# Attention and two feed-forward blocks: the first block's second layer in seven products instead of eight

## The chip, the cores and the metric

The kernel runs on one core of a Trainium2 chip. The metric is the device time of one execution in microseconds; 961.36 us is the median of three runs (958.15, 961.36 and 961.68).

## The reference

Four batches of 448 tokens, 12 heads of 64: sigmoid attention gives x, 1792 tokens by 768. Two feed-forward blocks follow, all in float32.

```python
scores = scale * np.matmul(q, k.transpose(0, 1, 3, 2)) - np.log(S)
attn = 1.0 / (1.0 + np.exp(-scores))
x = np.matmul(attn, v)                       # reshaped to 1792 x 768
h = x @ moe_w_in                             # layer 1: 768 -> 2048
g = h - np.tanh(h)
x = g @ moe_w_out                            # layer 2: 2048 -> 768
h = x @ moe2_w_in                            # layer 3: 768 -> 2048
g = np.maximum(h, 0.0) + alpha * np.minimum(h, 0.0)
out = g @ moe2_w_out                         # layer 4: 2048 -> 768
```

## The kernel before

**Numbers.** A float32 product is made of float16 halves: every operand is split into a high part, the value times a power of two rounded to float16, and a low part, what the rounding left. `split` (line 271) writes both: the high part on ACT or DVE, as the planner likes, the low part on DVE alone. Three matmuls (`PASSES`: high by high, high by low, low by high) stand for one. A matmul takes 128 by 128 weights and 448 columns of activations (one batch). The tokens are worked in two halves `sb` of 896.

**Weights.** They arrive as float64 words. `words` (line 311) makes float32 of a unit of six 128 by 128 tiles with three DVE instructions out of a `stage` tile that GpSimd's queue (POOL) loads; the halves go by POOL to a scratch in DRAM (`to_scratch`), and SyncE (SP) fetches them when PE wants them (`fetch`). Layers 1 and 2 (`w1`, `w2`) are converted unit by unit (`convert`). For layers 3 and 4 (`w3`, `w4`) `convert_quarter` (line 344) takes four units, the blocks 21, 22, 11 and 12 of one quarter `q` of the matrix, forms four sums on DVE (`tt`) and writes seven scratch tiles, since these layers use Strassen's method in Winograd's form: a 2 by 2 block product takes seven products instead of eight (`SEQ` is their order), the sums of activations being made by `entry` (line 591) and `exits` (line 674).

**Layers.** Layer 1: `product` adds up 36 matmuls into one of four PSUM tiles `ps0` to `ps3` in turn, and `bend` (line 551) makes g of it; its last reader of the PSUM tile is a COPY_PREDICATED on DVE. `lagged` runs half 0 ahead of half 1. After a half's sixteenth row a scale is formed from the maxima (`scale_of`), and `split_act` splits g into 16 tiles `sG`. Layer 2 has 12 products of 96 matmuls, each copied out of PSUM once by ACT and squared once for the scale. Layers 3 and 4 have 1008 matmuls each, layers 1 and 2 have 1152 each. Layer 4 writes three banks (`YB`) and three others (`ZB`) alternately; one of either three lies in `ps2`.

**Order.** `Plan` keeps every instruction as a node with a cost, an engine, what it reads and writes. `deadlines` works back from PE's fixed sequence, and `run` (line 104) places nodes engine by engine by that deadline, hands out 51 SBUF slots of 128 by 896 float32, and fixes the order; `window` and `keep` hold a node back. Costs (`act`, `vec`, `MM`, and `MB` for bytes moved) are constants of the program. Every engine then works through its own sequence and waits where an operand isn't there. All instructions go through one helper, so that the profile names line 210 for nearly all of them; they are told apart by operation, names and shape.

Of the kernel before, what the change touches and what calls it, by code (L numbers as in the profile page):

```python
# [19 lines left out]
T2 = 2 * S  # L20
# [20 lines left out]
LAG = 4  # L41
# [4 lines left out]
class Node:  # L46


    def __init__(self, n, engine, cost, emit, reads, writes, lat, window, keep):
        self.n, self.engine, self.cost, self.emit = n, engine, cost, emit  # L50
        self.touched = list(dict.fromkeys(r[0] for r in (*reads, *writes)))
        self.lat, self.window, self.keep = lat, window, keep
        self.before, self.after = set(), []
        self.late = self.end = None
        self.left, self.ready = 0, 0.0


class Plan:
# [3 lines left out]
    MB = 1.0 / 0.33  # L62
# [7 lines left out]
    def add(self, engine, cost, emit, reads=(), writes=(), lat=0.12, window=None, keep=1.0):  # L70
        node = Node(len(self.nodes), engine, cost, emit, reads, writes, lat, window, keep)
# [25 lines left out]
    def deadlines(self):  # L97
        total = sum(n.cost["T"] for n in self.nodes if n.engine == "T")
        for n in reversed(self.nodes):
            length = min(n.cost.values())  # L100
            ends = [a.late - (0.0 if n.engine == "T" and a.engine == "T" else n.lat) for a in n.after]
            n.late = min(ends, default=total + 8.0) - length - (n.cost.get("M", 0.0) * self.MB)

    def run(self):
# [20 lines left out]
        while done < len(self.nodes):  # L125
            picked = None
            base = order[turn].late if turn < len(order) else 1e9
            for e in engines:
# [10 lines left out]
                for n in waiting[e]:  # L139
# [5 lines left out]
                    key = n.late + (6.0 if len(n.engine) > 1 and e == "V" else 0.0)  # L145
# [79 lines left out]
def body(ctx: ExitStack, tc, qkd, vd, w1, w2, w3, w4, al, out):  # L225
# [8 lines left out]
               for m in (2, 3) for pr in range(1, 8) for q in range(NQ)}  # L234
    scratch.update({u: dr_pool.tile([128, 2 * UC], F16, name=f"scr_{u}") for u in range(2 * NU)})
# [35 lines left out]
    def split(dst, src, reads, scale, pick_dst, pick_src, n, regions, extra=(), ptr=0, keep=1.0):  # L271
# [9 lines left out]
        def low(e):  # L281
# [4 lines left out]
            [(dst, "h", r) for r in regions], keep=keep)  # L286
# [18 lines left out]
    def load_stage(i, queue):  # L305
# [3 lines left out]
        add(queue, {queue: 0.06 if queue == "S" else 0.6, "M": 0.786}, f, [], [(f"#stage{i % NSTAGE}",)])  # L309

    def words(i, name, after=()):
# [3 lines left out]
        def w():  # L315
# [5 lines left out]
            [*s, *after], whole(name), keep=8.0)  # L321
# [9 lines left out]
    def to_scratch(key, name, scale):  # L331
# [5 lines left out]
            parts(dst, (0,)), [("#scr", key)])  # L337
# [6 lines left out]
    def convert_quarter(m, q):  # L344
# [71 lines left out]
    def load_pair(i, halves=1):  # L416
        name = f"sqk{i}"
        n = T2 // halves
        for j in range(halves):
            add("S", {"S": 0.06, "M": 0.46 / halves},  # L420
                lambda e, j=j: SP.dma_start(out=slot(name)[:, j * n:(j + 1) * n], in_=qkd[i][:, j * n:(j + 1) * n]),
                [], [(name, j)] if halves == 2 else whole(name), window=60.0, keep=8.0)
# [6 lines left out]
    def load_values(g):  # L429
        add("S", {"S": 0.06, "M": 0.46}, lambda e: SP.dma_start(out=slot(f"sv{g}"), in_=vd[g]),  # L430
            [], [(f"sv{g}", 0)], window=60.0, keep=8.0)
# [60 lines left out]
    def weight_units(m, n0, nk):  # L492
        return sorted({n // UN for n in range(n0, n0 + nk)})

    turn = [0]

    def fetch_units(m, u, again):
        fetch((m if m < 2 else 1) * NU + u, f"sW{m},{u}")

    def product(m, n0, nk, act_of, sb, chunk):  # L500
# [3 lines left out]
        for c0 in range(0, nk, chunk):  # L504
            ks = range(c0, c0 + chunk)

            def f(e, ks=ks):
                for k in ks:
                    u, r = divmod(n0 + k, UN)
                    t = slot(f"sW{m},{u}").bitcast(F16)[:, 0:2 * UC]  # L510
                    w = t.rearrange("p (a k c) -> p a k c", a=2, k=UN)[:, :, r, :]
                    for i, j in PASSES:
                        for b in range(2):
                            PE.matmul(p[:, b, 0:S], w[:, i], act_of(k, sb, b)[1][:, j],
                                      start=(k == 0 and (i, j) == (0, 0)),
                                      stop=(k == nk - 1 and (i, j) == (1, 0)))
# [427 lines left out]
```

## Time and profile before

| | us |
|---|---|
| three runs | 958.15, 961.36, 961.68 |
| the profiled execution | 957.92 |
| its span, first to last instruction | 955.9 |
| layer 1, 2, 3, 4 begin | 131.4, 349.6, 567.9, 761.0 |

The profile is of one execution. A row by form gives the busy time of a group of like instructions and the mean of one; neighbours on an engine overlap a little, so that busy time divided by the count is what one more instruction costs. A window gives each engine's busy time in a stretch. The stretches of the layers follow from PE's sequence: 1008, 1008 and 1152 matmuls make up exactly the 3168 that the timeline has from 349.57 on.

### The profile page before, as it was taken

How to read it: one execution, taken by the hardware profiler on the slowest of the kernel's cores; microseconds unless marked ns; L12 is line 12 of the kernel's file. 1: busy time of each engine (PE TensorE's matmuls, PEld its weight loads, DVE VectorE, ACT ScalarE, POOL GpSimd, SP SyncE). 2: the span in 40 equal slices, each digit the busy share in tenths (PEclk: the TensorE clock that was granted, in tenths of full speed). 3: DMA queues.
4: the chain of work that ended last, by engine and by line, in shares of the span. 5: the costliest groups of instructions: out<-in, count | busy, mean ns of one | idle time of the engine just before them, and what ended most of it. 6: DMA issues, size and time to landing. Idle time of an engine off the chain costs nothing. (4 is left out here: it accounts for less than half of the span.)

```text
span 955.9 us, 13508 instructions
## 1 busy us (share of the span) xinstructions
PE 943.6 (99%) x5280; PEld 464.7 (49%) x5280; DVE 708.7 (74%) x878; ACT 593.0 (62%) x739; POOL 87.6 (9%) x163
## 2 busy tenths in 40 slices
PE   7999999999999999999999999999999999999998
PEld 2333345555555555555555555455555455555554
DVE  5779889999988999957999999643782479792000
ACT  7999859999999998512543347765663476271000
POOL 0011220011100000111223220100000000000000
PEclk9999999999999999999999999999999999999999
DMA  9962883455331123586768983733223345443441
GB/s 352 412 253 96 276 298 103 161 182 192 133 122 50 34 90 108 182 281 215 265 232 326 384 308 121 247 117 125 92 65 102 130 149 177 154 143 122 161 128 58
DMA packets 48287, 170.75 MB, mean 179 GB/s; under 512 B 6112, under 2 KB 9440, under 8 KB 48224
## 3 DMA queue, kind: packets, MB, share of 16 engines
q1 hardware_dynamic: 32544, 88.10, 27.8%
q0 software_dynamic: 15680, 81.80, 23.5%
q8 instruction: 41, 0.67, 0.3%
q14 instruction: 22, 0.18, 0.1%
HBM read 129.77 MB, written 40.11 MB: 178 GB/s over the span
## 5 line engine op out<-in xcount | busy, mean ns | idle before, releaser
L210 PE MATMUL ps<-slot,slot 128*128 128x448 f16 (+2 forms) x4704 | 890.8, 369 | 2.2 <-ACT slot L210 1.6
L210 PEld LDWEIGHTS <-slot 128*128 128x128 f16 (+2 forms) x4896 | 444.6, 98 | 448.1 <-issue 33.5
L210 ACT ACTIVATE slot<-slot 128x896 f32<-128x896 f32 (+3 forms) x193 | 171.9, 903 | 141.0 <-DVE slot L210 103.9
L210 ACT ACTIVATE slot<-slot,sc 128x896 f16<-128x896 f32 (+1 forms) x164 | 164.0, 1030 | 61.2 <-PE ps L210 23.8
L210 DVE SCALAR_TENSOR_TENSOR slot<-slot,sc,slot 128x896 f16<-128x896 f32 (+1 forms) x122 | 132.6, 1138 | 5.6 <-ACT slot L210 5.4
L210 DVE SCALAR_TENSOR_TENSOR slot<-slot,slot 128x768 f16<-128x768 f32 (+2 forms) x113 | 108.9, 977 | 30.4 <-ACT slot L210 28.5
L210 DVE SCALAR_TENSOR_TENSOR slot<-stage,slot 128x768 int32<-128x768 int32 x128 | 120.7, 956 | 1.6
L210 DVE SCALAR_TENSOR_TENSOR slot<-ps,sc,slot 128x896 f32<-128x896 f32 (+1 forms) x50 | 48.3, 978 | 90.2 <-ACT slot L210 47.4
L210 ACT ACTIVATE slot<-ps 128x896 f32<-128x896 f32 x64 | 57.4, 909 | 62.1 <-PE ps L210 42.2
L210 ACT ACTIVATE slot<-ps,sc 128x896 f32<-128x896 f32 (+1 forms) x56 | 46.7, 837 | 74.2 <-PE ps L210 72.2
L210 ACT ACTIVATE slot<-ps,cst 128x896 f32<-128x896 f32 x84 | 79.4, 1015 | 4.8 <-PE ps L210 4.0
L210 DVE TENSOR_TENSOR slot<-slot,slot 128x768 f32<-128x768 f32 (+2 forms) x82 | 73.9, 933 | 10.0 <-ACT slot L210 9.7
L210 DVE SCALAR_TENSOR_TENSOR slot<-slot,nalpha,slot 128x448 f32<-128x448 f32 x64 | 41.0, 681 | 40.0 <-ACT slot L210 40.0
L210 POOL DMA_DIRECT2D scr<-slot x88 | 48.4, 550 | 216.0 <-DVE slot L210 176.0
L210 ACT ACTIVATE slot<-slot,cst 128x896 f32<-128x896 f32 x64 | 66.4, 1040 | 1.8 <-DVE ps L210 0.5
L210 PE MATMUL ps<-slot 64*128 64x448 f16 (+1 forms) x576 | 57.4, 359 | 6.0 <-ACT slot L210 5.9
L210 POOL DMA_DIRECT2D stage<-w x60 | 34.0, 567 | 292.8 <-DVE slot L210 286.0
L210 DVE TENSOR_TENSOR slot<-ps,slot 128x896 f32<-128x896 f32 x24 | 26.1, 1088 | 37.4 <-ACT slot L210 25.7
L210 DVE TENSOR_SCALAR slot<-stage 128x768 int32<-128x768 int32 x64 | 35.4, 557 | 11.1 <-DMA scr<-slot 8.1
L210 PEld LDWEIGHTS ps<-slot,slot 128*64 128x64 f32 (+1 forms) x384 | 20.1, 135 | 38.6 <-issue 36.0
L210 DVE COPY_PREDICATED slot<-slot,ps 128x896 f32<-128x896 int32 x32 | 38.0, 1187 | 0.1
L210 DVE SCALAR_TENSOR_TENSOR ps<-ps,sc,slot 128x896 f32<-128x896 f32 x32 | 36.9, 1152 | 0.0
(22 smaller groups left out, 129.1 us busy)
## 6 DMA issues: line engine op xcount, KB each, us to landing
slot<-scr SPq DMA_DIRECT2D x160, 384.0 KB, 3.7
stage<-w POOLq DMA_DIRECT2D x60, 768.0 KB, 5.1
scr<-slot POOLq DMA_DIRECT2D x88, 384.0 KB, 5.1
slot<-qk SPq DMA_DIRECT2D x23, 448.0 KB, 9.0
slot<-v SPq DMA_DIRECT2D x12, 448.0 KB, 9.0
out_t<-slot SPq DMA_DIRECT2D x24, 224.0 KB, 2.3
stage<-w SPq DMA_DIRECT2D x4, 768.0 KB, 10.9
slot<-qk SPq DMA_DIRECT2D x2, 224.0 KB, 2.7
```

Source lines behind the costliest of these rows:

```text
L210: return lambda *args, **kw: self.tc.keep_in_program_order(f(*args, **kw))
```

## The change

Layer 2 takes the seven products. `w2` is laid out in blocks and converted by `convert_quarter(1, q)`, which writes 28 scratch tiles instead of 16; each half of the tokens fetches 28 instead of 16. For `w2` and `w3` the sums of weight blocks are no longer made on DVE: ACT negates a block in place (`negate`) and a DMA on POOL's queue adds one SBUF tile to another (`plus`, `accum_op`), 32 such DMAs; `w4` keeps DVE. `exits` now also serves g: 16 differences of blocks per half on DVE, and 28 split tiles instead of 16. `multiply_out` is layer 4's loop made a function that layer 2 uses too, with 1008 matmuls; out of PSUM go 12 half-size copies on ACT, 9 half-size additions on DVE and 12 half-size squares per half. A product of layer 1 now covers two rows of 128 features and one batch instead of one row and two batches. The planner gets longer latencies for DMAs, a slightly higher rate of bytes, and new windows and reserves.

```diff
-LAG = 4
+AHEAD = {1: (0, 1, 3, 0), 2: (19, 22, 0, 20), 3: (27, 50, 7, 42)}
+CHAIN = {1: 5, 2: 1, 3: 4}
+MOVED = (False, False)
+LAG, KEEP_W, KEEP_F, KEEP_P, WIN_F, WIN_O, WIN_P, SPARE_V, WIN_Q = 4, 6, 4, 7, 16, 31, 39, 12, 51
+WSUM = (True, True, False)
...
-    MB = 1.0 / 0.33
+    MB = 1.0 / 0.36
...
-                    key = n.late + (6.0 if len(n.engine) > 1 and e == "V" else 0.0)
+                    key = n.late + (SPARE_V if len(n.engine) > 1 and e == "V" else 0.0)
...
-                n.end = moved + 1.2
-            n.emit(e)
+                n.end = moved + n.lat
...
-        add(queue, {queue: 0.06 if queue == "S" else 0.6, "M": 0.786}, f, [], [(f"#stage{i % NSTAGE}",)])
+        add(queue, {queue: 0.06 if queue == "S" else 0.6, "M": 0.786}, f, [], [(f"#stage{i % NSTAGE}",)], lat=4.0)
...
-        def tt(out_, a, b, op):
-            add("V", {"V": vec(UC)},
-                lambda e: V.tensor_tensor(slot(out_)[:, 0:UC], slot(a)[:, 0:UC], slot(b)[:, 0:UC], op),
-                [*whole(a), *whole(b)], whole(out_))
+        def plus(out_, a, sign):
+            if WSUM[m - 1]:
+                add("G", {"G": 0.9, "M": 0.65},
+                    lambda e: G.dma_start(out=slot(out_)[:, 0:UC], in_=slot(a)[:, 0:UC], accum_op=ALU.add),
+                    whole(a), whole(out_), lat=5.0)
+            else:
+                add("V", {"V": vec(UC)},
+                    lambda e: V.tensor_tensor(slot(out_)[:, 0:UC], slot(out_)[:, 0:UC], slot(a)[:, 0:UC],
+                                              ALU.add if sign > 0 else ALU.subtract),
+                    whole(a), whole(out_))
+        def negate(a):
+            if WSUM[m - 1]:
+                add("A", {"A": act(UC)},
+                    lambda e: A.activation(slot(a)[:, 0:UC], slot(a)[:, 0:UC], AF.Copy, scale=-1.0), (), whole(a))
         def put(pr, name, scale=SW2):
-            to_scratch((m, pr, q), name, scale)
-        a21, a22, a11, a12, r = n_("21"), n_("22"), n_("11"), n_("12"), n_("r")
+            to_scratch((m, pr, q), name, scale, AHEAD[m][q])
...
-        words(first, a21, [("#scr", 2 * NU - 1 if not (m - 2 or q) else (m - (not q), 2, (q - 1) % NQ))])
+        words(first, a21, [("#scr", NU - 1 if m == 1 and not q else (m - (not q), CHAIN[m], (q - 1) % NQ))])
         words(first + 1, a22)
-        tt(r, a21, a22, ALU.add)
-        put(5, r)
-        put(4, a22, -SW2)
+        put(4, a22, -SW2 if m == 2 else SW2)
+        plus(a22, a21, 1)
+        put(5, a22)
         words(first + 2, a11)
-        tt(r, r, a11, ALU.subtract)
-        put(6, r)
-        tt(a21, a11, a21, ALU.subtract)
-        put(7, a21)
-        put(1, a11)
+        negate(a11)
+        turned = -SW2 if WSUM[m - 1] else SW2
+        plus(a22, a11, -1)
+        put(6, a22)
+        plus(a21, a11, -1)
+        put(7, a21, -SW2)
+        put(1, a11, turned)
         words(first + 3, a12)
-        tt(r, a12, r, ALU.subtract)
-        put(3, r)
-        put(2, a12)
-    fetched = [0]
+        negate(a12)
+        plus(a22, a12, -1)
+        put(3, a22, -SW2)
+        put(2, a12, turned)
...
-            [("#scr", key)], [(name, 0)], window=18.0, keep=6.0)
+            [("#scr", key)], [(name, 0)], window=WIN_F, keep=KEEP_F, lat=2.2)
...
-            scale_of(2 + sb, KF, sc[:, sb, 6:7], sc[:, sb, 7:8], 1.0, reads=s1)
-            for j in range(KF):
-                split_act(f"sG{j},{sb}", f"sg{j},{sb}", 2 + sb)
+            scale_of(2 + sb, KF, sc[:, sb, 6:7], sc[:, sb, 7:8], 1.0, ACT_EXP2, SW2, reads=s1)
+            exits(sb, 2 + sb, "G", "Q", MOVED[0])
...
-            sub(blk(1, 0, q), t2(q), blk(1, 0, q))
-            put(4, blk(1, 0, q), q)
+            less(t2(q), blk(1, 0, q), t2(q))
+            put(4, t2(q), q)
...
+                for e in range(3):
+                    add("T", {"T": 6 * MM}, lambda e_, e=e, f=f: f(e_, e),
+                        [(w, 0), *parts(src, (0,))], [region(bks[e])], lat=0.2)
+                    if q == NQ - 1:
+                        if pr == 1:
+                            copied(bks[e], e, 0, False)
+                        elif pr == 6:
+                            copied(bks[e], e, 1, False)
+                        elif pr == 7:
+                            copied(bks[e], 3 + e, 1, False)
+                        elif pr == 4:
+                            copied(bks[e], 3 + e, 0, True)
+                        elif pr == 3:
+                            added(bks[e], e, 1)
+            for e in (2, 0, 1):
+                if pr == 2:
+                    added(bks[e], e, 0)
+                if pr == 7:
+                    added(ZB[e], 3 + e, 1)
...
+        def measure(row, j):
+            col = 2 * row + j
+            add("A", {"A": act(S, acc=True)},
+                lambda e: A.activation(junk[:, 0:S], y_half(row, j), AF.Square, scale=SQ,
+                                       accum_out=mx[:, 4 + sb, col:col + 1]),
+                [(f"sy{row},{sb}", j)], [("junk",), (f"mx{4 + sb}", col)])
+        def copied(bk, row, j, last):
+            add("A", {"A": act(S, True)}, lambda e: A.activation(y_half(row, j), bank(bk), AF.Copy),
+                [region(bk)], [(f"sy{row},{sb}", j)])
+            if last:
+                measure(row, j)
+        def added(bk, row, j):
+            add("V", {"V": vec(S)},
+                lambda e: V.tensor_tensor(y_half(row, j), bank(bk), y_half(row, j), ALU.add),
+                [region(bk)], [(f"sy{row},{sb}", j)])
+            measure(row, j)
+        multiply_out(1, sb, "Q", copied, added)
...
-    for i in range(NU, 2 * NU):
-        convert(i)
...
+    for q in range(NQ):
+        convert_quarter(1, q)
...
-        for e in range(KD):
-            need(1 + sb, e * KF, KF)
-            k0 = product(1 + sb, e * KF, KF, of_g, sb, 2)
-            copy_of(k0, f"sy{e},{sb}")
-            add("A", {"A": act(T2, True, acc=True)},
-                lambda e_, k0=k0, sb=sb, e=e: A.activation(full(k0), full(k0), AF.Square, scale=SQ,
-                                                           accum_out=mx[:, 4 + sb, e:e + 1]),
-                [], [*banks(k0), (f"mx{4 + sb}", e)])
-        scale_of(4 + sb, KD, 1.0, inv_of(2 + sb), SQ, ACT_EXP2, SW2, reads=[(f"#sc{2 + sb}",)])
+        second_layer(sb)
+        scale_of(4 + sb, 2 * KD, 1.0, inv_of(2 + sb), SQ, ACT_EXP2, SW2, reads=[(f"#sc{2 + sb}",)])
...
-        "w1": tiles(moe_w_in), "w2": tiles(moe_w_out), "w3": blocks(moe2_w_in, 3, 2),
+        "w1": tiles(moe_w_in), "w2": blocks(moe_w_out, 2, 3), "w3": blocks(moe2_w_in, 3, 2),
```

DVE around layer 2's start, before: the last `bend`s of layer 1 as they let go of `ps1`, `ps2` and `ps3` (`slotN` are SBUF slots, `stageN` the words just loaded).

```order
L210 COPY_PREDICATED slot8_159<-slot32_183,ps1_213 128x896
L210 SCALAR_TENSOR_TENSOR slot14_165<-slot14_165,ps2_214 128x896
L210 SCALAR_TENSOR_TENSOR slot0_151<-slot0_151,ps3_215 128x896
L210 SCALAR_TENSOR_TENSOR slot4_155<-ps2_214,sc_210,slot14_165 128x896
L210 SCALAR_TENSOR_TENSOR ps2_214<-ps2_214,sc_210,slot3_154 128x2x448
L210 SCALAR_TENSOR_TENSOR slot13_164<-ps3_215,sc_210,slot0_151 128x896
L210 COPY_PREDICATED slot4_155<-slot9_160,ps2_214 128x896
L210 SCALAR_TENSOR_TENSOR ps3_215<-ps3_215,sc_210,slot12_163 128x2x448
L210 TENSOR_SCALAR slot3_154<-stage2_204 128x768
L210 COPY_PREDICATED slot13_164<-slot10_161,ps3_215 128x896
L210 SCALAR_TENSOR_TENSOR slot3_154<-stage2_204,slot3_154 128x768
L210 TENSOR_SCALAR slot10_161<-stage1_203 128x768
```

DVE at the same place, now: the releases of `ps0`, `ps1` and `ps2`.

```order
L215 COPY_PREDICATED slot45_208<-slot31_194,ps0_224 128x896
L215 SCALAR_TENSOR_TENSOR ps1_225<-ps1_225,sc_222,slot40_203 128x2x448
L215 SCALAR_TENSOR_TENSOR slot11_174<-slot11_174,ps2_226 128x896
L215 COPY_PREDICATED slot43_206<-slot5_168,ps1_225 128x896
L215 TENSOR_SCALAR slot30_193<-stage0_214 128x768
L215 TENSOR_SCALAR slot5_168<-stage3_217 128x768
L215 SCALAR_TENSOR_TENSOR slot32_195<-ps2_226,sc_222,slot11_174 128x896
L215 SCALAR_TENSOR_TENSOR slot30_193<-stage0_214,slot30_193 128x768
L215 SCALAR_TENSOR_TENSOR ps2_226<-ps2_226,sc_222,slot6_169 128x2x448
L215 SCALAR_TENSOR_TENSOR slot37_200<-slot20_183,sc_222,slot37_200 128x896
L215 COPY_PREDICATED slot32_195<-slot10_173,ps2_226 128x896
L215 SCALAR_TENSOR_TENSOR slot6_169<-slot6_169,ps3_227 128x896
```

Before, one instruction of word formation for `w3` stands between the last two releases. Now word formation for the last quarter of `w2` and a split of g stand between the releases, and layer 2's first three banks lie in `ps0`, `ps1` and `ps2`.

POOL at that place, before: two scales and the first tiles of `w3` (`scr2_p_q` is product p, quarter q).

```order
L210 ISA sc_210<-sc_210 128x1
L210 DMA scr_31_150<-slot4_155 128x1536
L210 ISA sc_210<-sc_210 128x1
L210 DMA stage2_204<-w3 128x1536
L210 DMA scr2_1_0_63<-slot0_151 128x1536
L210 DMA stage1_203<-w3 128x1536
L210 DMA stage0_202<-w3 128x1536
L210 DMA stage3_205<-w3 128x1536
```

POOL there now; a DMA from slot to slot is an accumulating one.

```order
L215 DMA slot4_167<-slot30_193 128x768
L215 DMA stage0_214<-w3 128x1536
L215 DMA stage3_217<-w3 128x1536
L215 DMA slot30_193<-slot1_164 128x768
L215 DMA scr1_2_3_70<-slot7_170 128x1536
L215 DMA slot4_167<-slot1_164 128x768
L215 DMA scr1_5_3_82<-slot37_200 128x1536
L215 DMA scr1_7_3_90<-slot7_170 128x1536
L215 DMA scr1_6_3_86<-slot1_164 128x1536
L215 DMA slot4_167<-slot5_168 128x768
L215 DMA scr1_3_3_74<-slot5_168 128x1536
```

The last quarter of `w2` (`scr1_p_3`) is now written around layer 2's start, with four accumulating DMAs and two loads of `w3` in the same queue; two of the accumulating ones write `slot4` in turn before product 6 can be split.

## Rows read from the trace of the kernel before

**Rows 1.** The page, part 1: busy us (share) and instructions.

```profile
PE 943.6 (99%) x5280; PEld 464.7 (49%) x5280; DVE 708.7 (74%) x878; ACT 593.0 (62%) x739; POOL 87.6 (9%) x163
```

**Rows 2.** The page, part 2: granted TensorE clock, 40 slices.

```profile
PEclk9999999999999999999999999999999999999999
```

**Rows 3.** Windows of layers 1 to 4: us, busy (count) by engine, PEclk, DMA share, GB/s.

```profile
131.40:349.50 218.10, 217.95 (x1152) 112.62 (x1151) 203.63 (x232) 199.68 (x238) 19.58 (x37) 1.00 0.38 130
349.50:567.90 218.40, 218.33 (x1155) 112.95 (x1155) 195.75 (x251) 97.06 (x127) 44.23 (x78) 1.00 0.69 247
567.90:761.00 193.10, 191.08 (x1008) 98.40 (x1007) 112.90 (x152) 114.65 (x155) 5.96 (x11) 1.00 0.40 132
761.00:955.90 194.90, 190.81 (x1009) 98.50 (x1007) 96.33 (x113) 70.39 (x88) 0.35 (x1) 1.00 0.43 136
```

**Rows 4.** Timeline of PE: start us, us, what; [idle before].

```profile
349.57 252.35 PE L210 MATMUL ps<-slot,slot 128*128 128x448 f16 x1332 [0.21 <-ACT slot L210]
...
754.16 197.65 PE L210 MATMUL ps<-slot,slot 128*128 128x448 f16 x1044 [1.01 <-ACT slot L210]
```

**Rows 5.** Groups by form, DVE, two of ACT, one of POOL: busy us, mean ns | idle before.

```profile
L210 DVE SCALAR_TENSOR_TENSOR slot<-slot,sc,slot 128x896 f16<-128x896 f32 x120 | 131.2, 1146 | 5.6 <-ACT slot L210 5.4
L210 DVE SCALAR_TENSOR_TENSOR slot<-stage,slot 128x768 int32<-128x768 int32 x128 | 120.7, 956 | 1.6
...
L210 ACT ACTIVATE slot<-slot,sc 128x896 f16<-128x896 f32 x98 | 97.0, 1033 | 50.0 <-PE ps L210 23.8 <-DVE slot L210 10.9 <-DVE sc L210 5.5
L210 DVE SCALAR_TENSOR_TENSOR slot<-slot,slot 128x768 f16<-128x768 f32 x88 | 82.8, 956 | 13.8 <-ACT slot L210 12.9
...
L210 ACT ACTIVATE slot<-slot 128x768 f16<-128x768 f32 x72 | 60.3, 840 | 102.2 <-DVE slot L210 73.9 <-issue 14.1 <-PE ps L210 11.2
...
L210 POOL DMA_DIRECT2D scr<-slot x88 | 48.4, 550 | 216.0 <-DVE slot L210 176.0 <-ACT slot L210 32.8 <-DMA slot<-v 2.1
...
L210 DVE COPY_PREDICATED slot<-slot,ps 128x896 f32<-128x896 int32 x32 | 38.0, 1187 | 0.1
L210 DVE SCALAR_TENSOR_TENSOR ps<-ps,sc,slot 128x896 f32<-128x896 f32 x32 | 36.9, 1152 | 0.0
L210 DVE SCALAR_TENSOR_TENSOR slot<-ps,sc,slot 128x896 f32<-128x896 f32 x32 | 36.7, 1146 | 8.3 <-ACT slot L210 8.0 <-DMA scr<-slot 0.2
L210 DVE TENSOR_SCALAR slot<-stage 128x768 int32<-128x768 int32 x64 | 35.4, 557 | 11.1 <-DMA scr<-slot 8.1 <-PE ps L210 2.4 <-DMA stage<-w 0.4
L210 DVE SCALAR_TENSOR_TENSOR slot<-slot,ps 128x896 f32<-128x896 f32 x32 | 34.4, 1076 | 1.9 <-ACT slot L210 1.8
...
L210 DVE TENSOR_TENSOR slot<-slot,slot 128x896 f32<-128x896 f32 x32 | 33.1, 1085 | 0.1
...
L210 DVE TENSOR_TENSOR slot<-slot,slot 128x768 f32<-128x768 f32 x32 | 30.2, 957 | 0.2
...
L210 DVE SCALAR_TENSOR_TENSOR slot<-ps,sc,slot 128x448 f32<-128x448 f32 x18 | 11.7, 680 | 81.9 <-PE ps L210 42.6 <-ACT slot L210 39.4
...
L210 DVE TENSOR_SCALAR slot<-slot 128x768 f16<-128x768 f32 x16 | 9.0, 560 | 1.0 <-PE ps L210 0.2
```

**Rows 6.** Window, the last 50 us of layer 1, columns as in 3.

```profile
300.00:350.00 50.00, 49.78 (x264) 25.69 (x263) 49.83 (x59) 48.54 (x57) 1.93 (x4) 1.00 0.20 64
```

**Rows 7.** Timeline near layer 2's start, DVE.

```profile
363.84 1.18 DVE L210 COPY_PREDICATED slot<-slot,ps 128x896 f32<-128x896 int32 x1
```

**Rows 8.** DMA issues: count, KB each, median us from issue to landing.

```profile
slot<-scr SPq DMA_DIRECT2D x160, 384.0 KB, 3.7
stage<-w POOLq DMA_DIRECT2D x60, 768.0 KB, 5.1
scr<-slot POOLq DMA_DIRECT2D x88, 384.0 KB, 5.1
```

**Rows 9.** Tile scr: landing times of its transfers.

```profile
DMA to landing us min/median/max: 2.6/4.0/10.7
```

**Rows 10.** Groups by form, PE, in layer 4 (766 to 956 us).

```profile
L210 PE MATMUL ps<-slot,slot 128*128 128x448 f16 x983 | 186.1, 352 | 0.0
```

More of the change, by code (lines that the diff above doesn't have):

```diff
@@ L101, in deadlines, with run @@
             ends = [a.late - (0.0 if n.engine == "T" and a.engine == "T" else n.lat) for a in n.after]
-            n.late = min(ends, default=total + 8.0) - length - (n.cost.get("M", 0.0) * self.MB)
-    def run(self):
+            n.late = min(ends, default=total + 8.0) - length - n.cost.get("M", 0.0) * self.MB - n.early
+    def run(self, dry=False):
         self.deadlines()
@@ L320, in words @@
             lambda e: V.tensor_scalar(w(), hi, 3, 0x3FFFFFFF, ALU.logical_shift_left, ALU.bitwise_and),
-            [*s, *after], whole(name), keep=8.0)
+            [*s, *after], whole(name), keep=KEEP_W)
         add("V", {"V": vec(UC)},
@@ L421, in load_pair @@
                 lambda e, j=j: SP.dma_start(out=slot(name)[:, j * n:(j + 1) * n], in_=qkd[i][:, j * n:(j + 1) * n]),
-                [], [(name, j)] if halves == 2 else whole(name), window=60.0, keep=8.0)
+                [], [(name, j)] if halves == 2 else whole(name), window=WIN_Q, keep=8.0, lat=2.2)
         for j in range(halves):
@@ L628, in multiply_in @@
         p = pst[k0]
-        w = f"sV{pr},{q},{sb}"
+        w = f"sv2,{pr},{q},{sb}"
         fetch((2, pr, q), w)
@@ new lines, in region, with multiply_out, f @@
+    def region(k):
+        return (f"ps{k[0]}", k[1])
+    def multiply_out(m, sb, P, copied, added):
+        for pr in SEQ:
+            bks = YB if pr in (1, 6, 7, 4) else ZB
+            for q in range(NQ):
+                w, src = f"sV{m},{pr},{q},{sb}", f"s{P}{pr},{q},{sb}"
+                fetch((m, pr, q), w)
+                def f(e_, e, w=w, src=src, pr=pr, q=q, bks=bks):
+                    wt = pair_of(slot(w)).rearrange("p a (k c) -> p a k c", k=UN)
+                    a = hl(slot(src))
+                    for c in range(2):
+                        for n, (x1, x2) in enumerate(PASSES):
+                            PE.matmul(bank(bks[e]), wt[:, x1, 2 * e + c], a[:, x2, c * S:(c + 1) * S],
+                                      start=pr in (1, 2, 5) and q == 0 and c == 0 and n == 0,
+                                      stop=q == NQ - 1 and c == 1 and n == 2, skip_group_check=True)
+                for e in range(3):
[17 more added lines that the diff above has]
+                    added(ZB[e], 3 + e, 1)
@@ new lines, in second_layer, with y_half @@
+    def second_layer(sb):
+        def y_half(row, j):
+            return two(slot(f"sy{row},{sb}"))[:, j]
+        def measure(row, j):
[15 more added lines that the diff above has]
+        multiply_out(1, sb, "Q", copied, added)
@@ new lines, in fourth_layer, with store, copied, added @@
+    def fourth_layer(sb):
+        iv = inv_of(6 + sb)
+        s1 = (f"#sc{6 + sb}",)
+        def store(row, j):
+            name = f"sH{row},{j},{sb}"
+            cols = slice(sb * T2 + j * S, sb * T2 + (j + 1) * S)
+            add("S", {"S": 0.06, "M": 0.23},
+                lambda e: SP.dma_start(out=out[row * 128:(row + 1) * 128, cols], in_=slot(name)[:, 0:S]),
+                [(name, 0)], [("out", row, sb, j)], lat=2.0)
+        def copied(bk, row, j, last):
+            name = f"sH{row},{j},{sb}"
+            add("A", {"A": act(S, True, 1)},
+                lambda e: A.activation(slot(name)[:, 0:S], bank(bk), AF.Copy, scale=iv),
+                [region(bk), s1], [(name, 0)])
+            if last:
+                store(row, j)
+        def added(bk, row, j):
+            name = f"sH{row},{j},{sb}"
+            add("V", {"V": vec(S, 1)},
+                lambda e: V.scalar_tensor_tensor(slot(name)[:, 0:S], bank(bk), iv, slot(name)[:, 0:S],
+                                                 ALU.mult, ALU.add),
+                [region(bk), s1], [(name, 0)])
+            store(row, j)
+        multiply_out(3, sb, "P", copied, added)
@@ L755, in body @@
                 split_act(f"sX{j},{b}", f"sx{j},{b}", sb)
+    for q in range(NQ):
+        convert_quarter(1, q)
     got = set()
[L759 to L767 removed]
+    for n, sb in lagged(KF, LAG):
+        fp, j = divmod(n, 2)
+        for u in (2 * fp, 2 * fp + 1):
+            if u not in got:
+                got.add(u)
+                fetch(u, f"sW{u}")
+        bend(fp, j, sb, product(fp, j, sb))
     for m in (2, 3):
@@ L894, in body @@
+        fourth_layer(sb)
     plan.run()
```

187 lines of the change are left out of this document (60 added, 127 removed).

## The prediction

> **What bounds the kernel now.** I read the page's busy shares first. PE is busy 943.6 of 955.9 us, DVE 708.7 [rows 1], and the clock stands at its upper level (2.4 GHz) in all forty slices [rows 2]. So the time is PE's row of matmuls plus its gaps. Then the windows by layer: PE is busy to within 0.2 us in layers 1 and 2, while DVE is busy 203.6 of 218.1 us in layer 1, 195.8 of 218.4 in layer 2, 112.9 of 193.1 in layer 3 and 96.3 of 194.9 in layer 4 [rows 3]. DVE, not PE's data, is the next limit, and in the first two layers it is near. The timeline of PE gives the price of a matmul: 252.35 us for 1332 and 197.65 for 1044, so 0.1893 us [rows 4].
>
> **PE's saving.** Layer 2 goes from 1152 to 1008 matmuls of one shape. 144 x 0.1893 = 27.3 us, all on the path, as PE has no gaps there to swallow it. The new loop is layer 4's, which runs at that price with no idle time [rows 10], so a slower matmul is not expected. Layer 1 keeps its 1152.
>
> **What DVE gets.** One more instruction costs busy time over count [rows 5]: 32 block differences at 1.034 = 33.1; 24 low halves of g at 1.093 = 26.2; 12 low halves of weights at 0.941 = 11.3; 9 high halves that the planner now gives to DVE at 0.5625 = 5.1; 18 half-size additions out of PSUM at 0.65 (those of layer 4) = 11.7; three further high halves, 1.9 (an estimate from the row of 0.5625). Off go w3's 16 weight sums at 0.944 = 15.1 (w2 had none; its 16 sums are new work of the DMAs). Sum 74.2. DVE's groups by form, 27 of them, add up to 745 us busy (the largest is 131.2 [rows 5]) where DVE as a whole shows 708.7, so I take 0.951 of it: 70.6 us.
>
> Where does it go? Layer 1 has 14.5 us free and w2's share (11.3 + 5.1) x 0.951 = 15.6 asks for slightly more; the order puts w2's last quarter around layer 2's start, so this shows up as the first tight place, below. In layers 2 and 3 DVE was free for 102.8 us [rows 3]; off go 27.3 (the shorter layer) and 70.6, leaving 5. The order also moves some 21 us of w4's splits to stand in layer 4, which has 98 free. Room: about 26 us in 384. That is enough if DVE seldom waits; a static order at such a density is what the last 50 us of layer 1 are: DVE busy 49.83, PE 49.78 [rows 6], 0.22 lost. At that rate 384 us lose 1.7; I take **2 us**, from nothing to the 13 of the next paragraph.
>
> **First tight place: layer 2's start.** Before, layer 2 began with `ps0` and took 18 us per product; now it needs `ps0`, `ps1` and `ps2` within 12 matmuls, 2.3 us. `ps2` is filled by the last product but one, which ends 36 x 0.1893 = 6.8 us before layer 2, so it must be free 9.1 us after it is full. Before, that product ended at 349.6 - 6.8 = 342.8 and its COPY_PREDICATED at 363.84 + 1.18 = 365.0, 22.2 us later [rows 7]. With that lag PE would stand 13.1 us. But the order has the releases earlier. From the instruction on DVE that waits for a slot freed 55.7 us before layer 2 (294 matmuls), to the release of `ps2`, PE has 58.0 us of work. DVE has 68 instructions there: 9 COPY_PREDICATED at 1.1875, 9 PSUM updates at 1.153, 9 products out of PSUM at 1.147, 8 first steps at 1.075, 7 word steps at 0.943 and 4 at 0.553, 4 differences at 1.034, 4 low halves at 0.941 and 3 at 1.093, 2 high halves at 0.5625, nine short ones (2.0): 63.1 [rows 5], times 0.951 = 60.0. DVE is 2.0 us late even if it never waits. Nothing to gain (PE lost 0.2 there before); so 2.0 to 13.1. I take **2.5**, near the sum, as in rows 6 DVE waits for next to nothing.
>
> **Second: the accumulating DMAs.** No row shows one. The nearest are POOL's stores and loads: 384 KB and 768 KB both land after 5.1 us in the median [rows 8], at most 10.7 for a scratch transfer [rows 9]; from the first L = 5.1, from the last 10.7. In w2's last quarter the first accumulation into `slot4` is issued when DVE has finished a word step; the low half that reads it stands 9.2 us of DVE's work later. Off that: POOL's issue, 0.55, and the high half on ACT, 0.84 [rows 5]. It is hidden up to L = 7.8. The second one likewise has 9.8, hidden up to 8.4. Then **0 us** at 5.1, and 2L - 16.2 beyond (5.2 at 10.7): DVE is late there already, and every wait goes through. Queued behind those splits are layer 2's copies out of PSUM on ACT and its additions on DVE, for which PE waits. I take 5.1 since double the bytes cost no more; w3's four quarters have the same two in series but share the 26 us of room.
>
> A rule speaks for the other end. The Trainium skill, "Collectives: The Full Stack", section "The bandwidth ceiling: the fold count and why AG ≠ RS ≠ AR", says that an add in the DMA engines needs two source reads for each write, and that this halved a transfer's rate. An estimate by it is two plain landings, 10.2 us, for which the sum would be 4.2 us more; rows 8 show loads of twice the bytes landing no later, so I keep 5.1 and let the rival below carry it.
>
> **Third: changes of banks.** Layer 2 changes between `YB` and `ZB` twelve times, and 2.3 us after each the third bank lies in `ps2`, whose other half must have been copied or added by then. Layer 4 did the same with no idle time on PE [rows 10], but with ACT and DVE idle. Now a split on ACT (1.03) can be in front [rows 5]: the wait is one copy and that, inside 2.3. From 0 to 12 x 1.03; I take **1 us**.
>
> **Free.** ACT gets about 45 us (16 negations, 24 high halves, more small copies and squares); layer 2 has 121 free on it [rows 3]. POOL gets 44 DMAs, 24 us of issuing, where layer 2 shows 44 busy of 218. Their cover is w3 and w4's slack; without it they would come as late weights. DMA share in layer 2 was 0.69 at 247 GB/s [rows 3]: with 24 more fetches and 16 accumulations of two reads or one, and w4's transfers moved on to layer 3, I get some 300 GB/s, or 0.83: landings grow, not a bound.
>
> **Sum.** 957.9 - 27.3 + 2.5 + 0 + 1 + 2 = 936.1. The profiled execution lies low among the runs: its mean with the three is 959.8, 1.9 above. So **938 us**, 2.4% faster. A measurement of this kernel can tell about 0.5% (4.8 us) from no change.
>
> **Rivals.**
> - *Accumulations land late.* L = 10.7 gives 5.2 more at layer 2's start; w3's four quarters ask 4 x 5.2 = 21, inside 26. 943; with the banks' bound, 955. For it: the add has two sources, and layer 2 has DMA queues at 0.83. Against: rows 8. Also here, at 949: `ps2` freed with the old lag (10.6 more).
> - *They hold DVE so long that it becomes slower than before.* DVE works in its order, so an addition into `slot4` that has not landed stops everything behind it. With x = 2L - 16.2 the loss is x + 4x - 26 once w3's quarters have used up the room, and the saving left is 27.3 - 5.5 = 21.8: gone at x = 9.6, L = 12.9. At L = 15 (three of today's landings) x is 13.8 and the time 938 + 13.8 + 55.2 - 26 = 981. For it: 32 such DMAs and the density of DVE. Against: 12.9 is beyond the longest landing on record here.
> - *No change: the saving is lost to DVE.* In layer 3 DVE was idle for 80 us while it had little to do, waiting for others. If 48 us of such waits remain where there is room for 26, PE loses 22: 960. Against: rows 6, where DVE at that density waits for nothing.
> - *The sevens hide all else.* No stall anywhere, the old gaps of 2 us too: 957.9 - 27.3 - 2 + 1.9 = 930.
>
> **How the numbers follow.** Forecast (931 to 944) 0.62; better than that, 0.05; late accumulations or the old lag (944 to 956), 0.18; no change 0.07; slower 0.08. To leave out no more than 0.2, the range goes from 930 to 953: below it a part of the second, above it the last two and the tail of the third. Faster than 956.6: 0.85; within 0.5%: 0.07; slower than 966.2: 0.08.
>
> **What would show it.** PE's matmul row of layer 2 counts 1008 in about 191 us and 4176 in the group of 128-by-128 shapes. PE's idle time before matmuls released by ACT and DVE grows from 2.2 to about 8 us, most of it at layer 2's start by a COPY_PREDICATED of `ps2`. The accumulating DMAs' median landing is near 5 us; if above 8, ACT and DVE show waits on slot-from-slot DMAs near layer 2's start. DVE is busy about 779 us, above 90% from layer 1 to the end of layer 3. I am wrong if PE's gaps in layers 2 and 3 add up to over 15 us, or if the gaps come from fetches.

## The result and the profile after

The changed kernel takes 931.63 us (median of 931.04, 931.25, 932.02 and 932.16), the kernel before 960.08 beside it: a ratio of 0.9704, 95% interval 0.9681 to 0.9728, 3.0% faster. The profiled execution took 931.04 us, 26.9 less than that of before.

Page of the changed kernel, parts 1 and 2, answering [rows 1, 2]; then the largest PE group and the three DVE groups that grew most, answering [rows 5] (columns as there).

```profile
PE 916.1 (99%) x5136; PEld 450.6 (48%) x5136; DVE 776.2 (84%) x961; ACT 632.6 (68%) x814; POOL 122.6 (13%) x207
PEclk9999999999999999999999999999999999999999
```

```profile
L215 PE MATMUL ps<-slot,slot 128*128 128x448 f16 x4176 | 790.8, 352 | 3.5 <-DVE slot L215 2.3 <-ACT slot L215 1.0
...
L215 DVE SCALAR_TENSOR_TENSOR slot<-slot,sc,slot 128x896 f16<-128x896 f32 x144 | 160.5, 1143 | 30.8 <-ACT slot L215 30.6
...
L215 DVE SCALAR_TENSOR_TENSOR slot<-slot,slot 128x768 f16<-128x768 f32 x100 | 94.1, 950 | 12.1 <-ACT slot L215 9.1 <-PE ps L215 2.2
L215 DVE TENSOR_TENSOR slot<-slot,slot 128x896 f32<-128x896 f32 x64 | 67.5, 1081 | 0.1
```

PE lost 144 matmuls and 27.5 us. DVE gained 67.5 us and PE still waits for it only once, 2.3 us. The windows of layers 1 to 4 show where DVE's new work went; columns as in [rows 3].

```profile
131.40:349.00 217.60, 217.60 (x1152) 112.56 (x1151) 207.50 (x240) 203.51 (x247) 33.64 (x55) 1.00 0.50 158
349.00:542.20 193.20, 190.86 (x1009) 98.51 (x1007) 183.51 (x224) 114.70 (x170) 36.25 (x57) 1.00 0.76 247
542.20:734.00 191.80, 190.79 (x1009) 98.62 (x1008) 170.36 (x233) 125.72 (x170) 34.45 (x56) 1.00 0.77 263
734.00:929.30 195.30, 191.07 (x1010) 98.52 (x1007) 116.81 (x135) 78.56 (x97) 1.96 (x4) 1.00 0.43 141
```

DVE is busy 95, 95 and 89% of layers 1 to 3 (before: 93, 90 and 58%), and PE's gaps in each of them are 2.4 us at most. PE's timeline, start, length, [idle before], shows both gaps, at layer 2's start and 7 us before layer 4; under it DVE ahead of the first. The COPY_PREDICATED of 352.42 releases `ps2`.

```profile
353.64 372.61 PE L215 MATMUL ps<-slot,slot 128*128 128x448 f16 x1968 [2.34 <-DVE slot L215]
727.26 197.96 PE L215 MATMUL ps<-slot,slot 128*128 128x448 f16 x1044 [1.00 <-ACT slot L215]
```

```profile
350.30 1.17 DVE L215 SCALAR_TENSOR_TENSOR ps<-ps,sc,slot 128x896 f32<-128x896 f32 x1
351.36 1.16 DVE L215 SCALAR_TENSOR_TENSOR slot<-slot,sc,slot 128x896 f16<-128x896 f32 x1
352.42 1.17 DVE L215 COPY_PREDICATED slot<-slot,ps 128x896 f32<-128x896 int32 x1
```

The DMAs, as in [rows 8]. The accumulating ones are in the last row: they land after 7.9 us, where plain stores of the same size take 5.2.

```profile
stage<-w POOLq DMA_DIRECT2D x60, 768.0 KB, 6.3
scr<-slot POOLq DMA_DIRECT2D x100, 384.0 KB, 5.2
slot<-slot POOLq DMA_DIRECT2D x32, 384.0 KB, 7.9
```

### The profile page after: what moved, and what is told of

Its sections match the earlier page's. It is cut to its first block, busy times and chain, and to the rows that moved or that the text cites. A ratio compares the mean times of both kernels' runs of the same rounds, so it can differ in the third digit from the quotient of the medians.

```text
span 929.3 us, 13532 instructions
## 1 busy us (share of the span) xinstructions
PE 916.1 (99%) x5136; PEld 450.6 (48%) x5136; DVE 776.2 (84%) x961; ACT 632.6 (68%) x814; POOL 122.6 (13%) x207
## 4 chain that ended last, share of the span: by engine, by line
PE 96%; DVE 1%; ACT 1%; DMA 1%; issue 0%; SPq 0%; ACTq 0%
PE ps L215 96%; DVE slot L215 1%; ACT slot L215 1%; DMA slot<-qk 1%; DVE ps L215 0%; SPq L215 0%; ACTq L215 0%
## 5 line engine op out<-in xcount | busy, mean ns | idle before, releaser
L215 PE MATMUL ps<-slot,slot 128*128 128x448 f16 (+2 forms) x4560 | 863.3, 369 | 3.5 <-DVE slot L215 2.3
L215 PEld LDWEIGHTS <-slot 128*128 128x128 f16 (+2 forms) x4752 | 430.4, 98 | 435.7 <-issue 33.2
L215 ACT ACTIVATE slot<-slot,sc 128x896 f16<-128x896 f32 (+1 forms) x185 | 187.6, 1032 | 70.4 <-PE ps L215 34.7
L215 ACT ACTIVATE slot<-slot 128x896 f32<-128x896 f32 (+4 forms) x211 | 185.7, 895 | 72.2 <-DVE slot L215 55.6
L215 DVE SCALAR_TENSOR_TENSOR slot<-slot,sc,slot 128x896 f16<-128x896 f32 (+1 forms) x146 | 161.6, 1137 | 30.8 <-ACT slot L215 30.6
L215 ACT ACTIVATE slot<-ps 128x896 f32<-128x896 f32 (+1 forms) x76 | 59.3, 792 | 50.9 <-PE ps L215 44.2
L215 DVE TENSOR_TENSOR slot<-slot,slot 128x896 f32<-128x896 f32 (+2 forms) x98 | 92.9, 974 | 0.3
L215 DVE SCALAR_TENSOR_TENSOR slot<-slot,nalpha,slot 128x448 f32<-128x448 f32 x64 | 41.6, 677 | 10.9 <-ACT slot L215 10.8
L215 DVE TENSOR_TENSOR slot<-ps,slot 128x896 f32<-128x896 f32 (+1 forms) x42 | 36.8, 884 | 5.7 <-PE ps L215 3.9
L215 ACT ACTIVATE junk<-slot 128x448 f16<-128x448 f32 (+1 forms) x36 | 25.4, 706 | 20.4 <-DVE slot L215 19.9
L215 POOL DMA_DIRECT2D slot<-slot x32 | 29.3, 925 | 75.3 <-DVE slot L215 48.2
L215 PEld LDWEIGHTS ps<-slot,slot 128*64 128x64 f32 (+1 forms) x384 | 20.1, 135 | 38.6 <-issue 36.4
```

What stands on the lines that cost most here:

```text
L215: return lambda *args, **kw: self.tc.keep_in_program_order(f(*args, **kw))
```

## The experiments

### What each part is worth

The change has three parts: seven products, sums by DMAs, longer DMA times in the scheduler. They were taken apart.

**The DMA times alone, on the kernel before.** `MB` is 1/0.36, and each DMA has the latency that the change gives it.

```diff
-                n.end = moved + 1.2
+                n.end = moved + n.lat
```

> The kernel before with the scheduler's longer DMA times alone (0.36 MB a microsecond; 4.0 us for POOL's, 2.2 for SP's after the bytes). Theory (PE has 2 us of gaps there, so nothing can be won, and DVE has room): 960, within 2. Rival (the earlier issues take slots and DVE's turns from layer 1's bends): 964 or more.

957.24 us, ratio 0.9967 (0.9949 to 0.9984): about 3 us gained, slightly more than the theory allows. PE's idle time before the layers' matmuls fell from 2.2 to 1.0 us; where the rest comes from was not traced.

**Seven products, sums on DVE, old DMA times.**

```diff
-WSUM = (True, True, False)
+WSUM = (False, False, False)
-    MB = 1.0 / 0.36
+    MB = 1.0 / 0.33
-                n.end = moved + n.lat
+                n.end = moved + 1.2
```

> All weight sums on DVE and the scheduler's old DMA times: the changed kernel without the second and third part of its change. With the new times this is 941.4, with accumulating DMAs and the old times 968. Theory (the longer times are needed only because a sum now waits for a DMA): 941, within 4. Rival (loads, stores and fetches need them as well at this density of DVE): 950 or more, with PE waits that go back to stage loads and scratch.

965.99 us, 1.0062 (1.0038 to 1.0085): slightly slower than before. The theory fell, and the rival holds.

**The changed kernel with the old DMA times** (the last two of these edits).

> The changed kernel with the scheduler's old DMA times alone (1.2 us after the bytes, 0.33 MB a microsecond; everything else as changed, the planner orders anew). Theory (the longer times only put the fetches and loads nearer to what they take, and the engines' orders have room for that): 931, within 2. Rival (what is planned with 1.2 us and lands after 4 to 8 us makes DVE, ACT or PE wait in their fixed order): 938 or more, with waits on slot-from-scratch or slot-from-slot DMAs in the PE row.

968.00 us, 1.0065 (1.0039 to 1.0091). The rival's time holds, and by far. Its waits stand elsewhere than it said: PE waits for DVE (22.2 us) and ACT (8.3), and it is those two that wait for DMAs.

**The changed kernel with all sums on DVE** (the first of these edits).

> The changed kernel with all weight sums on DVE again (the planner orders anew): 32 sums of about 0.944 us, 30 us more for DVE, and no accumulating DMA. Theory (DVE's room is what the accumulating DMAs buy): in layer 1 the changed kernel has 10.5 us of DVE free and w2's 16 sums ask for 15, so layer 2 starts about 4 us later than now (its stall grows from 2.3 to about 6), while w3's 16 sums go into the 31 us free in layers 2 and 3: 935 us, 933 to 942. Rival (room to spare in both layers, the DMAs buy nothing): 931, within 1.

941.45 us, 0.9793 (0.9757 to 0.9828): the theory's number, at the upper end of its range. Its places fit less well: the stall at layer 2's start grew to 4.4 us (0.60 and 3.79) and not to 6, and PE's other gaps, 5.6 us, lie mostly later in layer 2 (1.41, 1.63 and 1.04). So:

| products | sums of w2 and w3 | old DMA times | new DMA times |
|---|---|---|---|
| eight (w2 has no sums) | DVE | 960.1 | 957.2 |
| seven | DVE | 966.0 | 941.4 |
| seven | DMAs | 968.0 | 931.6 |

The seven products alone lose 6 us; with the new times they gain 16, and the DMAs' sums another 10. The waits for DMAs from 131 to 735 us point to how. Columns: waited for, us in total, times, longest. First seven products, DVE sums, old times; then the same with new times; then DMA sums with old times; then the changed kernel; last, the kernel before.

```profile
ACT slot L215 <- DMA scr<-slot: 20.1, 9, 5.3
...
DVE slot L215 <- DMA scr<-slot: 6.2, 6, 2.1
```

```profile
ACT slot L215 <- DMA scr<-slot: 1.8, 1, 1.8
```

```profile
POOL slot L215 <- DMA slot<-slot: 24.3, 4, 10.9
...
ACT slot L215 <- DMA slot<-slot: 19.0, 9, 3.6
ACT slot L215 <- DMA scr<-slot: 15.8, 9, 4.5
```

```profile
ACT slot L215 <- DMA scr<-slot: 5.3, 2, 4.1
...
ACT slot L215 <- DMA slot<-slot: 3.3, 3, 2.0
```

```profile
ACT slot L210 <- DMA scr<-slot: 25.5, 12, 11.2
```

ACT waits for stores because a slot is handed out again before its store has landed: the old plan has a store done 3.2 us after its issue if nothing is ahead of it (0.8 to start, 1.2 for the bytes, 1.2 after them), and the stores of these two runs land after 4.7 and 5.7 us in the median. One stall of PE with DMA sums and old times can be followed back, the 4.55 us that end at 369.81: DVE's steps ahead of it start when a store lands (start, length, what).

```profile
358.97 5.52 DMA scr<-slot
...
367.67 2.11 DVE slot L215 x2
...
369.81 0.53 PE ps L215
```

All waits of ACT and DVE for DMAs add up to 27.2 us with DVE sums and old times and to 2.3 with new ones, 24.9 less, and the time differs by 24.5. With DMA sums it is 40.7 against 8.6, 32.1 less for 36.4. The time itself is made of PE's gaps, 17.5 and 27.1 us fewer with the new times, and of slower matmuls behind long gaps (last section), 7.4 and 10.3; that the waits of the other two engines add up to nearly the same was not followed wait by wait. In the kernel before the same two engines waited 31.1 us for DMAs and PE lost 2.2 in all, with DVE busy 74%; with the new times they waited 3.5, for the 3 us that were gained. The two kernels with old times keep the change's other constants (`AHEAD`, `CHAIN`, windows); what constants chosen for the old times would reach was not tried.

### Layer 2's start

**Less work for DVE.** Second and third word steps of w2's last quarter left out, order kept.

```diff
+            lambda e: None if 28 <= i < 32 else V.scalar_tensor_tensor(
...
```

> Same order, but the second and third word step of w2's last quarter are left out (those weights are thereby not put together): eight instructions, five of them ahead of the release of ps2 for which PE waits 2.3 us at layer 2's start, 4.5 us of DVE's work. Theory (the sum of DVE's work sets that release): the stall falls from 2.34 us to 0, and the time by 2.3, to 928.7. Rival (ACT, busy 57.2 of the 60.7 us ahead of it, or the fixed chain from product to release sets it): 1.5 us or more of the stall stay, and the time is 930.5 or more.

932.46 us, 0.9701 (0.9657 to 0.9745). The stall is 2.09 us, so my theory, that the sum alone sets the release, fell. The 60 us ahead of the release, first in the changed kernel with ACT's last high half, then here, with DVE's last two rows:

```profile
293.00:353.70 60.70, 58.36 (x310) 30.09 (x308) 59.47 (x71) 57.24 (x70) 5.02 (x9) 1.00 0.35 117
```

```profile
350.04 1.03 ACT L215 ACTIVATE slot<-slot,sc 128x896 f16<-128x896 f32 x1
```

```profile
293.00:353.20 60.20, 58.14 (x308) 29.94 (x307) 55.77 (x66) 56.73 (x70) 6.88 (x12) 1.00 0.37 117
```

```profile
350.94 1.15 DVE L215 SCALAR_TENSOR_TENSOR slot<-slot,sc,slot 128x896 f16<-128x896 f32 x1 [0.50 <-ACT slot L215]
352.01 1.17 DVE L215 COPY_PREDICATED slot<-slot,ps 128x896 f32<-128x896 int32 x1
```

DVE's work shrank by 3.7 us and its idle time grew by 3.2: it now waits, at last for ACT's high half, for a low half that stands ahead of the release. In the changed kernel that high half ended at 351.07, only 0.29 us before DVE came to the low half (351.36). So two things hold the release at nearly the same time, DVE's work and ACT's half, and less of the first alone gained 0.25 us.

**The release first.** Same plan, the last two steps of `ps2`'s bend moved ahead of that low half and a word step.

```diff
...
+    for names in (("ps2", "st7,0,1"), ("ps2", "su7,0,1")):
+        seq.insert(k, seq.pop(place(*names)[0]))
...
```

> Same plan as the changed kernel, but on DVE the PSUM update and the COPY_PREDICATED of ps2's last bend stand ahead of the word step and of the low half that were mixed in between them (0.87 and 1.06 us from start to start). Theory (the order on DVE within the bend's last steps sets the release of ps2, not the sum of DVE's work): the stall at layer 2's start falls from 2.34 us to about 0.4, time 929.1. Rival (ACT's steps of the bend set it): the stall stays at 1.5 or more, time 930 to 931.

Three executions took 931.26 to 932.15 us, no gain. A fourth, the profiled one, took 2496.02: its matmuls took more than twice their time (758 ns in the mean for 352), while DVE's and ACT's instructions took what they always do; why was not found. A further execution gives the trace:

> The same kernel as in e5_release_first, for a trace of its own: its other runs there, 931.3 to 932.2, are not below the changed kernel's. Theory (the order on DVE sets the release of ps2): stall 0.4 us at layer 2's start, and what it gives is lost at another place. Rival (ACT's steps set it): the stall stays at 1.5 or more.

932.17 us. The stall is 0.58 us, close to what the theory says. The word step and the low half now behind the release are also 1.9 us of DVE's work, and the low half is the one that can wait for ACT, so this run does not tell order, work and ACT's half apart. A new stall of 1.59 us stands 21.7 us later; under PE's two rows the chain that ends in it (start, length, what).

```profile
353.00 21.73 PE L215 MATMUL ps<-slot,slot 128*128 128x448 f16 x114 [0.58 <-DVE slot L215]
376.32 351.06 PE L215 MATMUL ps<-slot,slot 128*128 128x448 f16 x1854 [1.59 <-DMA slot<-scr]
```

```profile
357.35 4.05 DMA slot<-slot
...
362.29 0.88 POOL slot L215
...
364.93 6.73 DMA scr<-slot
...
371.68 4.59 DMA slot<-scr
...
376.32 3.77 PE ps L215 x19
```

PE's gaps, 3.3 us against 3.5, stay. What is late next is w2's last quarter: an accumulation lands, the next is issued, the store takes 6.73 and the fetch 4.59. In the changed kernel no such stall shows; there the stall of 2.34 brings PE to this place 1.8 us later. This edit puts a word step of that quarter later, so not all of the 1.59 need be there without it.

**Other banks.** The first four products without `ps2`; layer 4 uses the same banks, and the planner orders anew.

```diff
-    YB = ((0, 0), (1, 0), (2, 0))
-    ZB = ((3, 0), (3, 1), (2, 1))
+    YB = ((0, 0), (1, 0), (1, 1))
+    ZB = ((3, 0), (3, 1), (2, 0))
```

> Other banks for the output blocks of layers 2 and 4: YB lies in ps0 and both halves of ps1, ZB in both halves of ps3 and one of ps2 (the planner orders anew), so the first four products of layer 2 need no ps2. Theory: the stall of 2.34 us at layer 2's start goes and none takes its place, 928.7. Rival (two blocks of YB in one tile make the third wait for the copy of the second at the bank changes): six changes of up to 1 us, 931 to 935.

929.98 us, 0.9681 (0.9664 to 0.9698). The stall is gone, no bank change waits, and the fetch costs 0.48:

```profile
373.50 6.79 PE L215 MATMUL ps<-slot,slot 128*128 128x448 f16 x35 [0.48 <-DMA slot<-scr]
```

PE's gaps before these matmuls are 1.8 us. It is the best version tried, but only 1.6 us below the changed kernel, less than the 0.5% that can be told.

### The accumulating DMAs

**Plain copies.**

```diff
-G.dma_start(out=slot(out_)[:, 0:UC], in_=slot(a)[:, 0:UC], accum_op=ALU.add)
+G.dma_start(out=slot(out_)[:, 0:UC], in_=slot(a)[:, 0:UC])
```

> The 32 accumulating DMAs become plain copies from slot to slot of the same size, in the same order; the sums of weights are thereby left out. Theory (the second read and the addition are what lengthen them): the landing falls from 7.9 to about 5.2 us, that of the stores of 384 KB, and POOL's issue from 0.88 to 0.55. Rival (the queue and the way from slot to slot do it, at that place of the program): the landing stays at 7 to 8. Time in both: 931, within 2, since the landing is hidden.

931.39 us (one execution). Landing 5.7 and POOL's issue 0.584, against 7.9 and 0.925 with the addition: the theory in the main. But a store of the same size landed after 4.3 us in this run (5.2 in the changed kernel), so a plain copy from slot to slot still takes longer than a store. The DMA row and POOL's group here, then POOL's group of the changed kernel:

```profile
slot<-slot POOLq DMA_DIRECT2D x32, 384.0 KB, 5.7
```

```profile
L215 POOL DMA_DIRECT2D slot<-slot x32 | 18.7, 584 | 73.3 <-DVE slot L215 46.5 <-ACT slot L215 21.4 <-issue 2.6
```

```profile
L215 POOL DMA_DIRECT2D slot<-slot x32 | 29.3, 925 | 75.3 <-DVE slot L215 48.2 <-ACT slot L215 21.1 <-issue 2.1
```

The addition makes a copy's landing 1.4 times as long in this pair; over the runs with this order on POOL the accumulating DMAs' median is 7.1 to 7.9, so 1.2 to 1.4. The Trainium skill, "Collectives: The Full Stack", section "The bandwidth ceiling: the fold count and why AG ≠ RS ≠ AR", has a ring's ReduceScatter at half AllGather's rate because its add needs two source reads. If that held for the whole landing here, 5.7 would become an estimated 11.4; these rows show 7.9.

**Each twice.**

```diff
...
+                               for _ in range(2)],
...
```

> Every accumulating DMA is issued twice, one behind the other, in the order of the changed kernel, so that the addend counts twice and a sum lands after about 16 us instead of 7.9. Theory (the prediction's price, hidden up to 7.8 and then 2L - 16.2 at layer 2's start and once more for each quarter of w3, less 26 of room): x = 15.6, loss 15.6 + 62 - 26 = 52, so 983. Rival (the order leaves more slack than I read from it, or a wait on DVE lets the queue behind catch up): a loss below 20, 931 to 951.

1051.53 us, far above both. POOL itself waits for the first of each pair, 210.9 us in all, and its loads and stores queue behind:

```profile
L215 POOL DMA_DIRECT2D slot<-slot x64 | 59.4, 947 | 288.4 <-DMA slot<-slot 210.9
```

So it prices a blocked POOL, which I had not thought of, more than a late sum.

**Two stores ahead of each.**

```diff
...
+                    lambda e, x=next(late): [G.dma_start(out=x[k], in_=slot(a)[:, 0:UC]) for k in range(2)]
...
```

> Ahead of each accumulating DMA two stores of the same 384 KB of its addend go into POOL's DMA queue (to memory that nothing reads), same order otherwise, so a sum lands later without POOL waiting for it: L of 12 to 13 in place of 7.9, and 64 more issues of 0.55 us on POOL. Theory (the prediction's price of a late sum, x = 2L - 16.2, once at layer 2's start and once for each quarter of w3, less 26 of room): x = 8 to 10, loss 13 to 23, 944 to 954. Rival (the readers stand late enough, or later work catches up): 931 to 935.

971.45 us, although the landing grew only to 10.4. The edit does not keep POOL from waiting, as it was meant to: from 131 to 760 us POOL waited 40.8 us for DMAs (changed kernel: 10.6). My price gives x = 4.6 there and 943. PE's group, ACT's wait for the sums (3.3 us in the changed kernel), and one wait of another kind:

```profile
L215 PE MATMUL ps<-slot,slot 128*128 128x448 f16 x4176 | 800.1, 355 | 35.0 <-ACT slot L215 19.1 <-DVE slot L215 9.0 <-DMA slot<-scr 6.9
```

```profile
ACT slot L215 <- DMA slot<-slot: 25.3, 9, 7.2
```

```profile
587.49 1.22 DVE L215 TENSOR_SCALAR sc<-sc 128x1 f32<-128x1 f32 x7 [12.63 <-POOL sc L215]
```

Of 31.5 us more gaps on PE, 12.9 are one stall near layer 3's start: the scale of layer 2's second half stands on POOL behind the stores that I added and the DMAs between them, for some of which POOL waits. The other 18.6 us hold the late sums, but also late fetches (6.9), POOL's 36 us of added issues and its waits. So the run is no clean measure of a late sum, and its price was not settled.

### DVE's room

The third word step of each tile of `w3` and `w4` is done twice, order kept.

```diff
...
+                       for _ in range(2 if i >= 2 * NU else 1)],
```

> Same order as the changed kernel, but the third word step of each tile of w3 and w4 is done twice (the second time changes nothing): 32 more DVE instructions of 0.95 us, 28 us of DVE's time in layers 2 to 4, where DVE is free for 31 us in layers 2 and 3 and 78 in layer 4. Theory (the room on DVE can be filled, as the prediction assumed): less than 4 us lost, 931 to 935. Rival (DVE's idle time is waiting for others, so work put into its order goes to PE): half or more of the 28 arrives, 945 to 960.

955.10 us, 0.9948 (0.9931 to 0.9965): 23.5 of the 28 us arrive, the rival's case. In the profiled execution 16.9 us of that are gaps and 7.6 slower matmuls (last section).

```profile
L215 PE MATMUL ps<-slot,slot 128*128 128x448 f16 x4176 | 798.4, 354 | 20.4 <-DVE slot L215 15.3 <-ACT slot L215 4.9
```

DVE's 31 free us in layers 2 and 3 are waits of its fixed order; work put into that order came out on PE. A new order can use some of them: with all sums on DVE and the planner ordering anew, DVE is busy 95% of layer 3 and PE loses 1.0 us; here, with DVE at 92%, it loses 10.9. Layer 3 there, then here, columns as in [rows 3]; DVE has 11 us more to do there than in the changed kernel, and 18 here.

```profile
552.30:744.00 191.70, 190.69 (x1009) 98.53 (x1007) 181.76 (x247) 126.33 (x171) 31.42 (x53) 1.00 0.73 256
```

```profile
553.50:758.70 205.20, 194.28 (x1010) 99.22 (x1008) 187.93 (x253) 123.65 (x170) 36.59 (x58) 0.98 0.73 245
```

## Why the prediction held, and where its reasons did not

The forecast was 938, the range 930 to 953; measured 931.6, at the edge of the rival without stalls.

- **PE's saving**, 27.3: PE's group lost 27.5. Right, and it is the whole gain.
- **What DVE gets**, 70.6: 67.5. Right.
- **First tight place**, 2.5: 2.34, at the place and by the instruction named. DVE's work ahead of the release was 59.47 us where I had 60.0, and its waits 1.2 where I took 0.5. But the work is not the only thing that holds the release: with 3.7 us less of it the stall was still 2.09, with the low half and a word step behind it 0.58. My sum left out ACT's high half, done only 0.29 us before DVE needs it, and so it could not say what a remedy is worth.
- **Accumulating DMAs**, 0 at L = 5.1: 0, but L was 7.9, so that the 0 came by luck: hidden up to 7.8 and 8.4 was no margin at all. The chain they stand in, w2's last quarter, is the next to be late at that place (0.5 us with the other banks, 1.6 with the release first). The stores stayed at 5.2 and the loads went from 5.1 to 6.3.
- **Bank changes**, 1: no wait. **Density**, 2: none. **Scale**, 1.9: the profiled execution was 0.6 below the median. The layers' old gaps shrank from 2.2 to 1.2. With 1.3 of the scale, these four make 5.3 of the 6.4 us between 938 and 931.6.
- **Room of 26 us** was the step that failed unseen. It carried two rivals: late sums at 943 for L = 10.7, and a loss against before only from L = 12.9. At 10.4 the time was 971, not all of it through the sums, and 28 us more on DVE cost 23.5 where I had room for 26. The changed kernel has no stall there because its order was planned for this work; more work fits only where the order is made for it, as layer 3 with all sums on DVE shows. That late sums are dearer than I said follows from this, but no run shows it by itself. Nor is 12.9 beyond every landing: it is for the layers of the kernel before (10.7 at most), but loads in its first 131 us took up to 14.5, and one transfer on POOL's queue in the changed kernel took 17.4.
- **Free**: ACT got 39.6 us where I had 45. POOL got 35.0 where I had 24, since an accumulating DMA takes 0.925 us to issue and not 0.55. None of it shows on PE.
- **What I costed nowhere** are the longer DMA times. I read the order, which already had them, and never asked what the plan would be without. Taken out, the change is 968, slower than before: in size the rival "they hold DVE", but mostly through waits of ACT, for sums and for slots whose stores had not landed.

## What to carry to other kernels

Free time of an engine in a fixed order is not room: ask which wait each piece of it is, and whether anything can be moved into it without moving a reader. When a planner gives out buffers, its times for DMAs should come from landings in the trace: here a plan with too short times for all DMAs (a store done 3.2 us after its issue, where it lands after about 5) lost the whole gain. Dense engines make this dear: in the kernel before, with DVE busy 74%, 27.6 us fewer waits for DMAs went with 3 us of time; with seven products, 24.9 and 32.1 us fewer went with 24.5 and 36.4. Where a stall is removed, the trace of the next version names what comes behind it, here up to 1.6 us of a DMA chain.

## What the runs showed of the hardware

A long gap on PE costs more than itself. In the changed kernel with old DMA times PE stands 5.74 us and later 4.55; windows around them, columns as in [rows 3], the clock third from the end.

```profile
362.87:365.27 2.40, 2.39 (x6) 0.84 (x6) 1.60 (x2) 2.40 (x4) 0.00 (x0) 0.50 0.42 169
...
369.81:375.00 5.19, 5.18 (x15) 2.08 (x15) 5.19 (x7) 4.03 (x5) 0.00 (x0) 0.50 0.01 3
375.00:400.00 25.00, 25.00 (x133) 12.92 (x132) 22.95 (x26) 12.52 (x16) 2.88 (x5) 1.00 0.52 158
```

At 0.50 (1.2 GHz) a matmul takes 0.35 to 0.40 us, at 1.00 (2.4 GHz) 0.189. After the gap of 2.34 us in the changed kernel the clock stayed at 1.00:

```profile
353.64:358.00 4.36, 4.36 (x24) 2.25 (x24) 4.36 (x5) 4.25 (x6) 1.43 (x2) 1.00 0.14 26
```

In two other runs 3.99 us after a gap of 3.79 (all sums on DVE) show 0.58 in the mean, and 3.52 us after one of 3.66 (doubled steps) 0.50.

So 27.1 us more of gaps came with 10.3 more of busy time with old DMA times, 31.5 with 9.3 in the late sums, 16.9 with 7.6 in the doubled steps. My rivals' prices counted the gaps alone.
